# A joint text and image attention block: the text's transposes, text gate and residual moved

## The chip, the core and the metric

The kernel runs on one core of a Trainium2 chip. The core has a matrix engine (TensorE, PE in the profile, with its weight loads as PEld), a vector engine (VectorE, DVE), a scalar engine (ScalarE, ACT), a general engine (GpSimd, POOL) and SyncE (SP), which here only issues DMAs. Sixteen DMA engines move data between device memory and the on-chip memory SBUF; TensorE writes its sums to a second on-chip memory, PSUM. The metric is the time of one execution on the device in microseconds, as the median of several runs.

## The reference

There are 2 batches, each with 256 image tokens and 32 text tokens of width D = 1152. Both streams are normalised and modulated by vectors that come from a condition `c`; they attend to one another jointly; each has an output projection, a gate and a residual. Everything is bf16.

```
mod_i = silu(c) @ wmod_img ; mod_t = silu(c) @ wmod_txt     # shift, scale, gate: the first 3 of 6 blocks of D
hi = layernorm(x_img) * (1 + sci) + shi
ht = layernorm(x_txt) * (1 + sct) + sht
q, k, v = concat(ht @ wqkv_txt, hi @ wqkv_img)              # along the tokens, each of q, k, v
a = softmax(q k^T * D**-0.5) v ;  at, ai = split(a)
out_i = x_img + gai * (ai @ wo_img)
out_t = x_txt + gat * (at @ wo_txt)
```

## The kernel before, in words

D is cut into KT = 9 blocks of 128 rows (index kt or dt). Image tokens form four tiles of 128 (`NIT`), text tokens of both batches together form 64 rows (`NTT`). Fourteen weight blocks of D x D pass through five slots (`w0` to `w4`) in an order written out by hand: `load_w` brings a block in one DMA, `load_rows` in several, cut at rows of 128. All these loads are issued by SyncE, in program order, and each waits until the last reader of its slot is done. `late_loads` issues the last five blocks: image gate, text value, image output (slot 4, rows cut at 3 and 6), text gate, text output (slot 1, cut at row 5).

Most instructions are wrapped in `pin`, which keeps an engine's instructions in program order; those that are not wrapped may be placed by the scheduler.

The order of the work on TensorE is: scale rows and image transposes, image values (`v_open`), shift rows, the image's Q (`qk_img`, block 0) and K (block 1) with hooks at given column blocks j, then the text's Q and K (`qk_txt`), scores, the gate row of the image (`img_gate`), the text's values (`v_txt`), transposes of the softmax, attention (`attn_pair`), and the outputs (`out_img` for four image tiles, `out_txt`).

What the change touches:

- **Text normalisation and transposes.** In the hook at j = 3 of Q, ScalarE takes the text's sums (lines 422 and 423), then `txt_norm` writes the normalised text to `xn_t` in two pieces, 640 and 512 columns, on partitions 0 to 63 and 64 to 127 (line 433). In the hook at j = 1 of K, `txt_transposes` has TensorE transpose five blocks of 128x128 into PSUM (`tr`, line 64), and ScalarE copies them to `xT_t` in two copies (line 441). Between the two hooks VectorE forms the text's shift from 18 long operations on `acc_sh` (lines 451 and 453). `shift_blocks` reduces it, TensorE folds it at j = 7 (`shift_fold`), and `txt_scale` and `txt_shift` make `hT_t`.
- **Gate rows.** `mod_rows` computes a gate's row for both batches in a tiled run: four column groups of 32 stand side by side on TensorE (`tile_position`), so four products run at once. `mod_row_out` has ScalarE copy the row (line 538) and POOL write it to device memory, `gsc` (line 540). POOL then reads it back, spread over the partitions: to `gb` for the image (line 554, `img_gate_spread`), to `gbf` for the text (line 564, in `txt_gate`).
- **Text residual.** `xf` holds the text residual in the layout of the text output; POOL loads it in two DMAs at the end of `img_gate_spread` (line 556).
- **Outputs.** `out_img` computes one image tile in chunks of 384 columns, nine products for each; VectorE multiplies by the gate (line 728) and adds the residual (line 729); a DMA stores the row. It takes a hook, `between`, that is called ahead of its second chunk. `out_txt` computes the text output in two halves of 2 x 288 columns, each with 18 products of 64 columns, two side by side; VectorE multiplies by `gbf` (line 745) and adds `xf` (line 746); two DMAs store it.

The PSUM pool `ps_mm` has six banks, `ps_tr` two. The order of the end is:

```
    C3 = (CH, CH, CH)
    out_img(0, C3)
    out_img(1, C3, between=txt_gate)
    out_img(2, C3)
    out_txt()
    out_img(3, (CH, CH, 224, 160), parts=(2 * CH, D - 160, D))
```

Of the kernel before, what the change touches and what calls it, by code (L numbers as in the profile page):

```python
# [8 lines left out]
ACT = mybir.ActivationFunctionType  # L9
# [5 lines left out]
def kernel(  # L15
# [26 lines left out]
    NTT = B * NT  # L42
    CH = 384
    NCH = D // CH
    VC = 288
# [5 lines left out]
    act = ctx.enter_context(tc.tile_pool(name="act", bufs=1))  # L51
    const = ctx.enter_context(tc.tile_pool(name="const", bufs=1))
    work = ctx.enter_context(tc.tile_pool(name="work", bufs=2))
    small = ctx.enter_context(tc.tile_pool(name="small", bufs=4))
    ps_mm = ctx.enter_context(tc.tile_pool(name="ps_mm", bufs=6, space=PSUM))
    ps_tr = ctx.enter_context(tc.tile_pool(name="ps_tr", bufs=2, space=PSUM))

    pin = tc.keep_in_program_order

    def mm(*a, **k):  # L60
        return pin(nc.tensor.matmul(*a, **k))  # L61

    def tr(*a, **k):
        return pin(nc.tensor.transpose(*a, **k))

    xt_flat = x_txt.rearrange("b n d -> (b n) d")
# [26 lines left out]
    def load_rows(slot, src, c0, cuts=(0, 3, 6)):  # L93
        t = wtile(slot)
        sv = wview(src, c0)
        for r0, r1 in zip(cuts, cuts[1:] + (KT,)):
            nc.sync.dma_start(t[:, r0:r1, :], sv[:, r0:r1, :])  # L97
        return t
# [45 lines left out]
    pb_all = act.tile([P, 2 * B + 1, PBW], bf, name="pb")  # L144
    pb_tiles = [pb_all[:, i, :] for i in range(2 * B)]
    pb_txt = pb_all[:, 2 * B, :]
    KH = (KT + 1) // 2
    xn_t = act.tile([P, KH * P], bf)
    nc.gpsimd.memset(pb_txt, 0.0)
    nc.gpsimd.memset(xn_t[NTT:P, (KT - KH) * P:KH * P], 0.0)  # L150
    nc.gpsimd.memset(pb_all[:, 0:2 * B, NTOK:PBW], 0.0)
    fold = const.tile([P, NGG, LW], bf)
    nc.vector.reduce_max(fold[:, 0, :], ident[:].rearrange("p (g l) -> p l g", g=NGG), axis=AX.X)
# [165 lines left out]
    t3, t0, t6 = [(x_tiles(k0, 1), k0, 1) for k0 in (3, 0, 6)]  # L319
# [39 lines left out]
    for kt in range(KT):  # L359
        for b in range(B):  # L360
            h = hT_i[:, kt, b * NI:(b + 1) * NI]
# [31 lines left out]
    gsc = tc.dram_tile([2, B, D], bf, name="mod_scratch")  # L393
# [20 lines left out]
    xT_t = act.tile([P, KT, NTT], bf)  # L414
# [14 lines left out]
    def txt_norm():  # L429
        rstd = ln_rstd(sm_t[0:NTT, 2:3], NTT, sign=-1.0)  # L430
        pin(nc.scalar.activation(sm_t[0:NTT, 1:2], sm_t[0:NTT, 0:1], ACT.Copy, scale=rstd[0:NTT, :]))
        for h, (c0, c1) in enumerate(((0, KH * P), (KH * P, D))):
            pin(nc.scalar.activation(xn_t[NTT * h:NTT * (h + 1), 0:c1 - c0], x_t[:, c0:c1], ACT.Identity,
                                     bias=sm_t[0:NTT, 1:2], scale=rstd[0:NTT, :]))

    def txt_transposes():
        tpt = ps_tr.tile([P, KH, 2, NTT], bf, tag="tr")
        for k in range(KH):
            tr(tpt[:, k].rearrange("p h t -> p (h t)"), xn_t[:, k * P:(k + 1) * P], ident[:])
        for h, (k0, k1) in enumerate(((0, KH), (KH, KT))):  # L440
            nc.scalar.copy(xT_t[:, k0:k1, :], tpt[:, 0:k1 - k0, h, :])

    acc_sh = act.tile([P, B, D], f32, tag="Bt")

# [91 lines left out]
    def mod_row_out(gps, si):  # L536
        g_sb = work.tile([P, VC], bf, tag="garow")
        pin(nc.scalar.copy(g_sb[:], gps[:]))
        for b in range(B):
            nc.gpsimd.dma_start(gsc[si, b, :].rearrange("(g j) -> g j", g=NGG), g_sb[b:P:32, :])  # L540

    gb = act.tile([P, B, D], bf, tag="Bt")
    gbf = act.tile([P, 2, VC], bf)
# [8 lines left out]
    def img_gate_spread():  # L552
        for b in range(B):
            pin(nc.gpsimd.dma_start(gb[:, b, :], gsc[0, b, :].partition_broadcast(P)))
        for g in range(2):
            pin(nc.gpsimd.dma_start(xf[64 * g:64 * g + NTT, :, :],
                                    xt_flat.rearrange("t (r g j) -> g t r j", r=2, g=2)[g]))

    def txt_gate():
        mod_row_out(mod_rows(w_ga_t), 1)  # L560
        for g in range(2):
            for b in range(B):
                r0 = 64 * g + 32 * b
                nc.gpsimd.dma_start(gbf[r0:r0 + NT, :, :],
                                    gsc[1, b, :].rearrange("(r g j) -> g r j", r=2, g=2)[g].partition_broadcast(NT))

    v_last()
    late = {}

    def late_loads():  # L570
        late["ga_i"] = load_w(0, wmod_img, 2 * D)
        shift_v_spread()
        late["v_t"] = load_w(2, wqkv_txt, 2 * D)
        late["o_i"] = load_rows(4, wo_img, 0)
        late["ga_t"] = load_w(3, wmod_txt, 2 * D)
        late["o_t"] = load_rows(1, wo_txt, 0, (0, 5))

    qk_img(w_q_i, 0, {0: (shift_part(0, 2),), 3: (txt_stats, shift_part(2, 4), txt_var, txt_norm),
                      5: (shift_part(4, 7),), 8: (shift_part(7, KT),)})
# [135 lines left out]
    def out_img(i, chunks, parts=None, between=None):  # L715
        b = i // TPB
        t0 = b * NTOK + qpos[b][i % TPB]
        o = work.tile([P, D], bf, tag="o")
        c0 = s0 = 0
        for n in chunks:  # L720
            if c0 and between:
                between = between()
# [5 lines left out]
            nc.vector.tensor_mul(tmp[:, 0:n], ps[:, 0:n], gb[:, b, c0:c0 + n])  # L728
            nc.vector.tensor_add(o[:, c0:c0 + n], tmp[:, 0:n], x_i[:, i, c0:c0 + n])  # L729
            c0 += n  # L730
            if parts is None and c0 == D or parts and c0 in parts:
                (nc.scalar if parts and c0 == D else nc.sync).dma_start(oi_v[b, i % TPB, :, s0:c0], o[:, s0:c0])
                s0 = c0

    def out_txt():
        of = work.tile([P, 2, VC], bf, tag="of", bufs=1)
        for r in range(2):
            ps = ps_mm.tile([P, VC], f32, tag="mm")
            for dt in range(KT):
                for g in range(2):  # L740
                    c0 = (2 * r + g) * VC
                    mm(ps[64 * g:64 * g + NTT, :], lhsT=aT[:, dt, NI:NI + NTT], rhs=w_o_t[:, dt, c0:c0 + VC],
                       start=(dt == 0), stop=(dt == KT - 1), tile_position=(0, 64 * g))
            tmp = work.tile([P, CH], bf, tag="tmp")
            nc.vector.tensor_mul(tmp[:, 0:VC], ps[:], gbf[:, r, :])
# [12 lines left out]

# [28 lines left out]
```

## Time and profile before

| what | value |
|---|---|
| median of 6 runs | 117.59 us (117.27 to 118.17) |
| the profiled execution: its time | 117.89 us |
| the profiled execution: its span | 115.7 us |
| TensorE busy | 110.4 us, 95% of the span |
| VectorE, ScalarE, POOL busy | 62%, 38%, 10% |
| moved by DMA | 41.02 MB, mean 355 GB/s |
| granted TensorE clock | full, throughout |

The span is the time from the first to the last instruction of the profiled execution; its time on the device has 2.2 us more, which lie around the span. Times in the views are counted from the start of the span. In a timeline a line has start, duration, engine, line of the kernel, operation, tiles as `out<-in`, shape and count; in brackets stands the idle time of the engine ahead of it and what ended it. A `q` behind an engine's name (SPq) marks an instruction of its queue, such as a DMA's issue.

### The profile page before, as it was taken

To read this page: it belongs to the slowest core of one execution; us is meant where nothing else is said; L and a number is where in the kernel's file an instruction comes from. 1 tells how busy PE (TensorE), PEld (TensorE's weight loads), DVE (VectorE), ACT (ScalarE), POOL (GpSimd) and SP (SyncE) were. 2 spreads that over 40 slices of the span, in tenths; PEclk is the share of its full clock that TensorE was granted. 3 is DMA by queue.
4 is the path that set the end of the run, shared out by engine and by line. 5 is a ranking of instruction groups with operands and counts; after the bars stand their busy time and mean duration, and the time that the engine had idled before them with its cause. 6 is when DMAs were issued, how large, how long until landed. Compare 5 with 4: busy or idle time off the path is not lost.

```text
span 115.7 us, 2579 instructions
## 1 busy us (share of the span) xinstructions
PE 110.4 (95%) x1078; PEld 63.8 (55%) x1078; DVE 72.1 (62%) x152; ACT 43.5 (38%) x93; POOL 12.1 (10%) x32
## 2 busy tenths in 40 slices
PE   4999899999999999999999999999999999999990
PEld 2246544445574444444744458887966665557670
DVE  3489492053879997999997040018768409556571
ACT  5799600042653259934323223244656400100000
POOL 7200000000000000000000000003441600407000
PEclk9999999999999999999999999999999999999999
DMA  3999999999999999999999999999999999961223
GB/s 118 355 356 397 401 405 411 411 412 413 410 401 410 305 386 413 408 415 352 412 410 408 411 408 408 335 408 406 415 398 410 407 419 368 410 263 41 112 51 102
DMA packets 18917, 41.02 MB, mean 355 GB/s; under 512 B 1323, under 2 KB 1851, under 8 KB 18907
## 3 DMA queue, kind: packets, MB, share of 16 engines
q1 hardware_dynamic: 18032, 39.85, 90.3%
q0 software_dynamic: 480, 0.89, 2.2%
q10 hardware_dynamic: 395, 0.12, 0.4%
q8 instruction: 8, 0.13, 0.4%
q14 instruction: 2, 0.02, 0.0%
HBM read 39.52 MB, written 1.34 MB: 353 GB/s over the span
## 4 chain that ended last, share of the span: by engine, by line
DMA 52%; SPq 17%; DVE 12%; PE 12%; ACT 2%; issue 2%
DMA t<-in_wmod_img_dram 23%; DMA t<-in_wmod_txt_dram 17%; SPq L97 15%; DMA x_t<-in_x_txt_dram 11%; PE ps L61 11%; DVE acc_sh L453 10%; SPq L108 1%; PE gps L61 1%; ACT junk L422 1%; ACT junk L423 1%; DVE tmp L728 1%; DVE o L729 1%; SPq L104 1%; ACT qkT L379 0%; DVE sm_t L426 0%
## 5 line engine op out<-in xcount | busy, mean ns | idle before, releaser
L61 PE MATMUL ps<-xT_i,t 128*128 128x512 bf16 x162 | 35.7, 379 | 0.0
L61 PEld LDWEIGHTS <-t 128*128 128x128 bf16 x333 | 21.0, 98 | 19.1 <-issue 0.5
L453 DVE SCALAR_TENSOR_TENSOR acc_sh<-t,sTf,acc_sh 128x1152 f32<-128x1152 bf16 x16 | 21.4, 1405 | 0.0
L61 PE MATMUL ps<-t,aT 128*128 128x384 bf16 (+3 forms) x153 | 20.3, 308 | 0.0
L61 PE MATMUL vps<-t,hS_i 128*128 128x512 bf16 (+1 forms) x108 | 17.9, 326 | 0.2 <-DVE hS_i L270 0.2
L61 PEld LDWEIGHTS <-aT 128*128 128x128 bf16 (+1 forms) x153 | 13.0, 101 | 7.1 <-issue 0.8
L61 PEld LDWEIGHTS <-hS_i 128*128 128x128 bf16 x108 | 9.1, 98 | 8.9 <-DVE hS_i L270 0.4
L381 ACT CAST qkT<-ps 128x512 bf16<-128x512 f32 (+2 forms) x11 | 6.1, 551 | 14.9 <-PE ps L61 13.5
L728 DVE TENSOR_TENSOR tmp<-ps,gb 128x384 bf16<-128x384 f32 (+2 forms) x13 | 6.8, 524 | 7.2 <-PE ps L61 7.2
L614 POOL TENSOR_SCALAR pb<-e,rs 128x32 bf16<-128x32 f32 (+1 forms) x5 | 2.3, 456 | 75.8 <-DVE rs L606 75.8
L61 PE MATMUL wps<-warm 128*128 128x512 bf16 x24 | 8.1, 498 | 1.5 <-DVE unit L128 1.5
L379 ACT ACTIVATE qkT<-ps 128x512 bf16<-128x512 f32 (+2 forms) x11 | 6.0, 559 | 7.3 <-PE ps L61 7.2
L178 DVE CAST v_i<-vps 128x512 bf16<-128x512 f32 x5 | 3.5, 691 | 8.0 <-PE vps L61 8.0
L594 DVE TENSOR_REDUCE nmx<-sps 128x1 f32<-128x288 f32 x4 | 1.8, 457 | 9.4 <-PE sps L61 9.4
L180 ACT CAST v_i<-vps 128x512 bf16<-128x512 f32 x4 | 2.3, 580 | 10.2 <-PE vps L61 10.2
L61 PEld LDWEIGHTS <-sT 128*32 128x32 bf16 x180 | 4.6, 96 | 1.9 <-issue 0.7
L61 PEld LDWEIGHTS <-warm 128*128 128x128 bf16 x25 | 2.7, 119 | 5.3 <-issue 2.9
L61 PE MATMUL gps<-t,sT 128*32 128x288 bf16 x144 | 5.2, 287 | 0.2 <-DMA t<-in_wmod_txt_dram 0.2
L61 PE MATMUL sps<-qkT 128*128 128x288 bf16 (+1 forms) x54 | 5.3, 287 | 0.0
L659 DVE TENSOR_SCALAR aT<-aps,svc 128x288 bf16<-128x288 f32 x9 | 4.3, 518 | 1.4 <-PE aps L61 1.4
L61 PE MATMUL aps<-pT,v_i 128*128 128x288 bf16 x36 | 5.1, 287 | 0.0
L729 DVE TENSOR_TENSOR o<-tmp,x_i 128x384 bf16<-128x384 bf16 (+2 forms) x13 | 4.4, 342 | 1.0 <-DMA out_dram<-o 0.6
(112 smaller groups left out, 105.4 us busy)
## 6 DMA issues: line engine op xcount, KB each, us to landing
t<-in_wqkv_txt_dram SPq DMA_DIRECT2D x3, 2592.0 KB, 11.9
t<-in_wmod_img_dram SPq DMA_DIRECT2D x2, 2592.0 KB, 15.4
t<-in_wmod_txt_dram SPq DMA_DIRECT2D x2, 2592.0 KB, 21.3
t<-in_wqkv_img_dram SPq DMA_DIRECT2D x3, 864.0 KB, 14.5
t<-in_wqkv_img_dram SPq DMA_DIRECT2D x1, 2592.0 KB, 16.8
t<-in_wo_img_dram SPq DMA_DIRECT2D x3, 864.0 KB, 12.8
t<-in_wqkv_img_dram SPq DMA_DIRECT2D x3, 576.0 KB, 8.7
t<-in_wmod_txt_dram SPq DMA_DIRECT2D x2, 864.0 KB, 13.4
```

The lines of the kernel that those rows point to most:

```text
L61: return pin(nc.tensor.matmul(*a, **k))
L97: nc.sync.dma_start(t[:, r0:r1, :], sv[:, r0:r1, :])
L178: nc.vector.tensor_copy(out_ap, in_ap)
L180: nc.scalar.copy(out_ap, in_ap)
L379: nc.scalar.mul(out_ap, in_ap, SCALE)
L381: nc.scalar.copy(out_ap, in_ap)
L453: pin(nc.vector.scalar_tensor_tensor(acc, w_sh_t[:, kt, :], col, acc, op0=ALU.mult, op1=ALU.add))
L594: pin(nc.vector.reduce_max(nmx[0:qn, :], sps[0:qn, :], axis=AX.X, negate=True))
L614: pin(nc.gpsimd.tensor_scalar(dst, src, rs[0:qn, :], 0.0, op0=ALU.mult, op1=ALU.add))
L659: nc.vector.tensor_scalar(dst, tiles[(b, dt)][:], bias, None, op0=ALU.add)
L728: nc.vector.tensor_mul(tmp[:, 0:n], ps[:, 0:n], gb[:, b, c0:c0 + n])
L729: nc.vector.tensor_add(o[:, c0:c0 + n], tmp[:, 0:n], x_i[:, i, c0:c0 + n])
```

## The change

It does four things. First, the text is no longer transposed by TensorE: `txt_norm` writes the normalised text in eight pieces of 32 tokens x 288 elements to four groups of 32 partitions, so that one VectorE transpose, which works in blocks of 32x32, gives `xT_t` directly. Second, the text gate is no longer called between chunks of image tile 1: `txt_gate` and `out_txt` now stand together between image tiles 1 and 2, and `out_txt` is cut into products of 32 columns (four side by side, as in the gate row), takes both halves over rows 0 to 4, then 5 and 6, then 7 and 8 of its weights, and accumulates in the two banks of `ps_tr`. The text output's weights are loaded with the same cuts, the image output's with one cut at row 5. Third, the text's gating and store (`out_txt_store`) come after image tile 2; its adds run on POOL. Fourth, POOL loads `xf` behind the write of the text's gate row. The operations concerned are wrapped in `pin`.

```diff
-    KH = (KT + 1) // 2
-    xn_t = act.tile([P, KH * P], bf)
+    xn_t = act.tile([P, KT, B, LW], bf)
     nc.gpsimd.memset(pb_txt, 0.0)
-    nc.gpsimd.memset(xn_t[NTT:P, (KT - KH) * P:KH * P], 0.0)
...
     def txt_norm():
...
-        for h, (c0, c1) in enumerate(((0, KH * P), (KH * P, D))):
-            pin(nc.scalar.activation(xn_t[NTT * h:NTT * (h + 1), 0:c1 - c0], x_t[:, c0:c1], ACT.Identity,
-                                     bias=sm_t[0:NTT, 1:2], scale=rstd[0:NTT, :]))
+        x_g = x_t[:].rearrange("p (k g l) -> p g k l", g=NGG, l=LW)
+        for g in range(NGG):
+            for b in range(B):
+                p0, p1 = NT * b, NT * (b + 1)
+                pin(nc.scalar.activation(xn_t[LW * g:LW * (g + 1), :, b, :], x_g[p0:p1, g], ACT.Identity,
+                                         bias=sm_t[p0:p1, 1:2], scale=rstd[p0:p1, :]))
 
     def txt_transposes():
-        tpt = ps_tr.tile([P, KH, 2, NTT], bf, tag="tr")
-        for k in range(KH):
-            tr(tpt[:, k].rearrange("p h t -> p (h t)"), xn_t[:, k * P:(k + 1) * P], ident[:])
-        for h, (k0, k1) in enumerate(((0, KH), (KH, KT))):
-            nc.scalar.copy(xT_t[:, k0:k1, :], tpt[:, 0:k1 - k0, h, :])
+        pin(nc.vector.transpose(xT_t[:].rearrange("p k t -> p (k t)"), xn_t[:].rearrange("p k b l -> p (k b l)")))
...
     def img_gate_spread():
         for b in range(B):
             pin(nc.gpsimd.dma_start(gb[:, b, :], gsc[0, b, :].partition_broadcast(P)))
+
+    def txt_gate():
+        mod_row_out(mod_rows(w_ga_t), 1)
         for g in range(2):
             pin(nc.gpsimd.dma_start(xf[64 * g:64 * g + NTT, :, :],
                                     xt_flat.rearrange("t (r g j) -> g t r j", r=2, g=2)[g]))
-
-    def txt_gate():
-        mod_row_out(mod_rows(w_ga_t), 1)
         for g in range(2):
             for b in range(B):
                 r0 = 64 * g + 32 * b
-                nc.gpsimd.dma_start(gbf[r0:r0 + NT, :, :],
+                pin(nc.gpsimd.dma_start(gbf[r0:r0 + NT, :, :],
...
-        late["o_i"] = load_rows(4, wo_img, 0)
+        late["o_i"] = load_rows(4, wo_img, 0, (0, 5))
         late["ga_t"] = load_w(3, wmod_txt, 2 * D)
-        late["o_t"] = load_rows(1, wo_txt, 0, (0, 5))
+        late["o_t"] = load_rows(1, wo_txt, 0, (0, 5, 7))
...
     def out_txt():
+        tiles = [ps_tr.tile([P, VC], f32, tag="tr", name="txo") for r in range(2)]
+        for d0, d1 in ((0, 5), (5, 7), (7, KT)):
+            for r, ps in enumerate(tiles):
+                for dt in range(d0, d1):
+                    for g in range(2):
+                        for b in range(B):
+                            c0, r0, t0 = (2 * r + g) * VC, 64 * g + NT * b, NI + NT * b
+                            mm(ps[r0:r0 + NT, :], lhsT=aT[:, dt, t0:t0 + NT], rhs=w_o_t[:, dt, c0:c0 + VC],
+                               start=(dt == 0), stop=(dt == KT - 1), tile_position=(0, r0))
+        return tiles
+
+    def out_txt_store(tiles):
         of = work.tile([P, 2, VC], bf, tag="of", bufs=1)
-        for r in range(2):
-            ps = ps_mm.tile([P, VC], f32, tag="mm")
-            for dt in range(KT):
-                for g in range(2):
-                    c0 = (2 * r + g) * VC
-                    mm(ps[64 * g:64 * g + NTT, :], lhsT=aT[:, dt, NI:NI + NTT], rhs=w_o_t[:, dt, c0:c0 + VC],
-                       start=(dt == 0), stop=(dt == KT - 1), tile_position=(0, 64 * g))
-            tmp = work.tile([P, CH], bf, tag="tmp")
-            nc.vector.tensor_mul(tmp[:, 0:VC], ps[:], gbf[:, r, :])
-            nc.vector.tensor_add(of[:, r, :], tmp[:, 0:VC], xf[:, r, :])
+        for r, ps in enumerate(tiles):
+            tmp = work.tile([P, CH], bf, tag="tmpt")
+            pin(nc.vector.tensor_mul(tmp[:, 0:VC], ps[:], gbf[:, r, :]))
+            pin(nc.gpsimd.tensor_add(of[:, r, :], tmp[:, 0:VC], xf[:, r, :]))
...
     out_img(0, C3)
-    out_img(1, C3, between=txt_gate)
+    out_img(1, C3)
+    txt_gate()
+    txt = out_txt()
     out_img(2, C3)
-    out_txt()
+    out_txt_store(txt)
     out_img(3, (CH, CH, 224, 160), parts=(2 * CH, D - 160, D))
```

More of the change, by code (lines that the diff above doesn't have):

```diff
@@ L539, in mod_row_out @@
         for b in range(B):
-            nc.gpsimd.dma_start(gsc[si, b, :].rearrange("(g j) -> g j", g=NGG), g_sb[b:P:32, :])
+            pin(nc.gpsimd.dma_start(gsc[si, b, :].rearrange("(g j) -> g j", g=NGG), g_sb[b:P:32, :]))
     gb = act.tile([P, B, D], bf, tag="Bt")
@@ L563, in txt_gate @@
                 r0 = 64 * g + 32 * b
-                nc.gpsimd.dma_start(gbf[r0:r0 + NT, :, :],
-                                    gsc[1, b, :].rearrange("(r g j) -> g r j", r=2, g=2)[g].partition_broadcast(NT))
+                pin(nc.gpsimd.dma_start(gbf[r0:r0 + NT, :, :],
+                                        gsc[1, b, :].rearrange("(r g j) -> g r j", r=2, g=2)[g].partition_broadcast(NT)))
     v_last()
@@ L713, with out_img @@
         attn_pair(*[[(b, dt) for dt in dts] for b in range(B)])
-    def out_img(i, chunks, parts=None, between=None):
+    def out_img(i, chunks, parts=None):
         b = i // TPB
@@ L720, in out_img @@
         for n in chunks:
-            if c0 and between:
-                between = between()
             ps = ps_mm.tile([P, CH], f32, tag="mm")
@@ L727, in out_img @@
             tmp = work.tile([P, CH], bf, tag="tmp")
-            nc.vector.tensor_mul(tmp[:, 0:n], ps[:, 0:n], gb[:, b, c0:c0 + n])
-            nc.vector.tensor_add(o[:, c0:c0 + n], tmp[:, 0:n], x_i[:, i, c0:c0 + n])
+            pin(nc.vector.tensor_mul(tmp[:, 0:n], ps[:, 0:n], gb[:, b, c0:c0 + n]))
+            pin(nc.vector.tensor_add(o[:, c0:c0 + n], tmp[:, 0:n], x_i[:, i, c0:c0 + n]))
             c0 += n
```

## The prediction

> **What bounds the kernel now.** I read the page's busy shares and DMA row first, then the timeline of each engine from the text normalisation on, then the DMA issues with their landings. One profiled execution carries the sum: its span is 115.7 us and its time 117.89 us, 0.30 above the median of the six runs (117.59), so I work out a difference in the span and apply it to the median. Half a per cent, 0.59 us, is about what a measurement of this kernel can tell from no change.
>
> ```profile
> PE 110.4 (95%) x1078; PEld 63.8 (55%) x1078; DVE 72.1 (62%) x152; ACT 43.5 (38%) x93; POOL 12.1 (10%) x32
> ...
> DMA  3999999999999999999999999999999999961223
> ```
>
> TensorE is busy for 95% of the span, and so are the DMA engines until the 35th slice, about 101 us. Both are bounds at once: a gain on TensorE counts only as far as the weights arrive earlier too. The text transposes and the tail on TensorE (start, duration), then the weight loads of the tail, and the evictions on ScalarE around the transposes:
>
> ```profile
> 52.58 0.44 PE L64 MATMUL tpt<-ident,xn_t 128*128 128x128 bf16 x5
> ...
> 54.90 1.29 PE L61 MATMUL gps<-t,shT 128*32 128x288 bf16 x36
> 56.01 1.28 PE L61 MATMUL gps<-t,sT 128*32 128x288 bf16 x36
> ...
> 90.80 6.01 PE L61 MATMUL ps<-t,aT 128*128 128x384 bf16 x36
> 97.02 1.29 PE L61 MATMUL gps<-t,sT 128*32 128x288 bf16 x36 [0.21 <-DMA t<-in_wmod_txt_dram]
> ```
>
> ```profile
> 98.24 7.10 PEld L61 LDWEIGHTS <-aT 128*128 128x128 bf16 x45 [0.24 <-issue]
> ...
> 105.66 2.10 PEld L61 LDWEIGHTS <-aT 128*64 128x64 bf16 x36 [0.32 <-issue]
> ...
> 107.98 4.39 PEld L61 LDWEIGHTS <-aT 128*128 128x128 bf16 x36 [0.23 <-issue]
> ```
>
> ```profile
> 50.84 0.60 ACT L379 ACTIVATE qkT<-ps 128x512 bf16<-128x512 f32 x1 [1.35 <-PE ps L61]
> 52.78 0.58 ACT L381 CAST qkT<-ps 128x512 bf16<-128x512 f32 x1 [1.34 <-PE ps L61]
> ...
> 55.00 0.58 ACT L381 CAST qkT<-ps 128x512 bf16<-128x512 f32 x1 [1.03 <-PE ps L61]
> ```
>
> An image product of 384 columns takes (6.01 - 0.33) / 35 = 0.162 us. A tiled run of 36 products of 32 columns, followed by another of its kind, takes 56.01 - 54.90 = 1.11 us. Each change of the tiling leaves a small hole: 45 products (7.30 us) fill the 7.42 us from 98.24 to 105.66, so 0.1 us a change. 36 products from 90.80 end at 96.64, so the text gate, at 97.02, waited some 0.28 us for its weights. ScalarE, waiting for TensorE, gives the pace of the Q and K blocks: 1.94 us from one to the next, 2.22 over the five transposes.
>
> The DMA issues (KB, then us to landing) and the end of VectorE:
>
> ```profile
> 79.17 6.09 SPq L97 DMA_DIRECT2D t<-in_wo_txt_dram  x1
> ...
> t<-in_wo_txt_dram SPq DMA_DIRECT2D x1, 1440.0 KB, 21.2
> t<-in_wo_txt_dram SPq DMA_DIRECT2D x1, 1152.0 KB, 17.9
> xf<-in_x_txt_dram POOLq DMA_DIRECT2D x2, 72.0 KB, 6.9
> gbf<-mod_scratch POOLq DMA_DIRECT2D x4, 36.0 KB, 2.1
> ```
>
> ```profile
> 99.05 1.21 POOL L540 DMA_DIRECT2D mod_scratch<-g_sb  x2 [7.49 <-ACT g_sb L538]
> 104.11 2.16 POOL L564 DMA_DIRECT2D gbf<-mod_scratch  x4 [3.85 <-DMA mod_scratch<-g_sb]
> ```
>
> ```profile
> 107.91 0.46 DVE L745 TENSOR_TENSOR tmp<-ps,gbf 128x288 bf16<-128x288 f32 x1 [1.20 <-DMA gbf<-mod_scratch]
> ...
> 111.12 0.56 DVE L728 TENSOR_TENSOR tmp<-ps,gb 128x384 bf16<-128x384 f32 x1 [0.51 <-PE ps L61]
> 111.71 0.36 DVE L729 TENSOR_TENSOR o<-tmp,x_i 128x384 bf16<-128x384 bf16 x1
> ...
> 112.96 0.24 DVE L729 TENSOR_TENSOR o<-tmp,x_i 128x160 bf16<-128x160 bf16 x1
> ```
>
> The first five row blocks of the text output's weights land at 79.17 + 21.2 = 100.4; the other four are issued behind them, at 79.17 + 6.09, and land 17.9 later at about 103.2, the last weights of the kernel. Today nobody waits for them: the text output starts at 105.66. VectorE ends at 113.20, right behind TensorE; then a store and the closing.
>
> **The change, part by part.**
>
> Transposes. TensorE loses five: 2.22 - 1.94, so 0.28 us goes. VectorE gains one 32x32-block transpose of 128x576 bf16. Not in the trace; the nearest row is the same operation on 128x288 f32, 0.47 us, so between 0.75 (half a fixed cost) and 0.95; I take 0.8. It stands behind the sums of acc_sh, so it delays the blocks' reduction, ready at 61.62 and used by TensorE at 66.94: 5.3 us of cover. Without it the 0.8 would stop TensorE. ScalarE loses two copies (0.71) and normalises in eight pieces of 288 instead of 640 and 512 elements: 0.92 and 0.81 us give 0.85 ns an element and 0.38 fixed, 0.62 a piece, 5.0 instead of 1.75 us. Behind it queue the evictions of the image's Q blocks: the one finished at 45.0 is read at about 51.5 instead of 47.7. There are six banks and a block takes 1.94 us, so its bank is wanted at 54.7; 3 us of cover. The memset on POOL at 2.3 us had no waiter. One limit: the value weights of the text are used at 81.81 and the DMA stream runs without a break, so part of the 0.28 may turn into a wait there; between 0 and 0.28, and the next step makes it indifferent.
>
> Loads. The image output's weights come in two DMAs instead of three, the text output's in three instead of two. Issue time on SP moves, but these DMAs land 13 to 21 us after issue in a backlog; zero. The residual xf (2 x 72 KB) leaves the stream at 90 us: at some 410 GB/s that is 0.36 us, so the last weights come at 102.8 instead of 103.2, the block rows 5 and 6 at 101.4 and rows 0 to 4 at 100.0.
>
> The tiled run. Image output 0 starts at 90.80 - 0.28 = 90.52; now 54 image products (8.76) precede the gate: 99.28, 0.10 for the change of tiling, gate from 99.38 (its weights long landed: the 0.28 of wait goes). Gate 1.11, text from 100.49. Text now has 72 products of 32 columns instead of 36 of 64; at the gate's pace 2.22 us. Both halves over rows 0 to 4 take 1.23 (101.72; landed 100.0), rows 5 and 6 take 0.49 (102.21; landed 101.4), and rows 7 and 8 are reached at 102.21 but land at 102.8. **TensorE waits 0.6 us there**; behind it stands image output 2. Then 0.05 + 0.49 + 0.10: image output 2 from 103.44, plus 27 x 0.162: image output 3 from 107.82 instead of 107.98. So of 0.28 + 0.28 + 0.2 for two changes of tiling, only 0.16 is left; the rest is the stall of the DMA stream, moved from the gate to the last weights.
>
> The gate row's trip. From the gate's last product to landed gbf it takes 9.5 us today (98.3 to 107.8). After: row copied at 101.1, two writes issued at 101.4 and 102.0, then xf's two issues (1.22 us on POOL) until 103.8, then gbf's four (3.7 us from first issue to last landing). The writes' landing decides. Row: 4.6 us under the weights' load; with an empty stream gbf needs 2.1. The Trainium skill, "DMA: Bandwidth & Descriptors", section "Anatomy of one DMA — SWDGE (gpsimd) path", gives about 2.0 us fixed. By the page, landing at 104.1 and gbf at 107.8; by the loaded row, 106.6 and 110.3. The load ends at 102.8, so I take 104.6 and gbf at 108.3. xf's issues lie inside that wait and cost nothing; if the wait were under 1.2 us they would.
>
> VectorE's end. The text multiplies now stand behind image output 2: its last eviction ends at about 108.96, so gbf at 108.3 is in time (today VectorE waited 1.20 for it). Two multiplies 0.96: 109.92; chunk 0 of image 3 (0.93) 110.85; chunk 1 is ready at 110.96; from there as today, 0.16 earlier: end at 113.04. (Image 2's row buffer waits for image 0's store, landed by 104.0 today; its first add now comes at 105.7, so nothing.) The text's two adds (0.62) leave VectorE for POOL: this pays for the later place. VectorE is full here, 4.03 us of work in 4.08.
>
> POOL's adds: 128x288 with two inputs, not in the trace. Its one-input rows are 0.47 us for 128x32 and 0.52 for 64x96, some 0.8 ns an element: at least 0.67. By two inputs at the page's pace (below) about 0.8 to 1.05. The text store waits for them (about 111.2), lands some 2.4 later at 113.6, before the last image store (114.8): zero by itself. But here a rule speaks against the change. Row first: VectorE's adds of 0.36 us at 104.9 and 106.4 kept that length while POOL issued DMAs. The Trainium skill, "SBUF — State Buffer", section "Who interferes with whom", says that a VectorE instruction with two SBUF inputs contends with a GpSimd instruction that reads SBUF, the first holding the shared ports to its end; "GPSIMD Engine Reference", section 3, has about 2.6 cycles an element for a two-input operation, 0.63 us on 288. The two adds would hold the port from 109.5 to E, and chunk 0's add (due 110.5) would wait until then; the end is E + 2.5. By the row: no cost, 113.04. By the rule with 0.8 us each, E = 111.1: 113.6. I take the row for the forecast, and keep 0 to +1.1.
>
> Sum: 0.16 earlier on TensorE and at the end: 115.7 - 0.15, so **117.59 - 0.15 = 117.44 us**.
>
> **The rivals.**
>
> 1. The forecast (36%): about 117.4, own range 117.0 to 117.9: the last weights are the bound before and after.
>
> 2. The last rows land early (24%): if they come by 102.2, TensorE gains the whole 0.28 + 0.28 + 0.2 = 0.8: image 3 from 107.2, VectorE's end at 112.4: 116.8; by half, 117.1. For it: the landing is that of the slowest engine, and gb's and xf's traffic at 93 to 97 us may have cost more than its bytes. Against: the DMA row has no idle slice to take up.
>
> 3. The port lock (26%), which ends slower: price E + 2.5 - 113.04. It decides from adds of 0.55 us each on: 0.7 each gives +0.4 against the forecast, 0.8 gives +0.6, 1.05 gives +1.1; so 117.8 to 118.5, at 118.0 for the middle. For it: the rule, and VectorE without slack. Against: no row shows it.
>
> 4. The gate row is late (14%): if the writes take their loaded 4.6 us, gbf lands at 110.3, and 0.96 + 0.93 + 0.92 + 0.66 + 0.56 behind it end at 114.3: 118.7. It decides from a landing of gbf at 109.0 on. Against: the load ends under way.
>
> **How the numbers follow.** The likeliest is 117.4. Faster by over 0.59 (under 117.0): three quarters of case 2 and a sixth of case 1, 0.24. Slower by over 0.59 (over 118.18): case 4, half of case 3 and a tenth of case 1, 0.31. Between: 0.45. The range takes case 2's full gain and most of case 3: 116.8 to 118.4; what is left out is mainly case 4.
>
> **What would show it.** Right: no product tpt; a wait of TensorE for in_wo_txt_dram inside the text output at about 102 us, 0.3 to 0.9 long; no wait of the gate for in_wmod_txt_dram; image 3 from about 107.8; VectorE's text multiplies straight behind image 2; a POOL add of 0.7 to 1.0 us. Case 2: no such wait. Case 3: an L729-like add of 128x384 well over 0.36 us beside POOL's. Case 4: the text multiply waits for gbf past 109. Wrong altogether: a wait of TensorE near 55 or 67 us (the normalisation or the transpose on the path), or text products slower than 0.03 us each.

## The result, and the profile after

The changed kernel takes 117.0 us (median of 34 runs, 116.21 to 118.19); the kernel before, on the same chips, 117.38 us (71 runs, 116.83 to 118.46). The ratio is 0.9962, with a 95% interval of 0.9948 to 0.9976: 0.44 us less (0.28 to 0.61). Measured once more, the same kernel gave 0.9943 (0.9911 to 0.9975, e11 below). Both intervals exclude 1, so there is a gain, and it is small: about the half per cent that the forecast took as what a measurement can tell.

The profiled execution of the new kernel has a span of 115.2 us and a time of 117.31. Its busy shares and the DMA row:

```profile
PE 109.5 (95%) x1109; PEld 63.1 (55%) x1109; DVE 72.2 (63%) x151; ACT 45.9 (40%) x97; POOL 13.2 (11%) x33
...
DMA  3999999999999999998999999999999999963043
```

TensorE lost 0.9 us of busy time and is still at 95%; the DMA engines are still full to the 35th slice. The text's normalisation and transpose on ScalarE and VectorE, then TensorE over the same time (timelines; start, duration):

```profile
46.10 5.09 ACT L434 ACTIVATE xn_t<-x_t,sm_t,rstd 32x288 bf16<-32x288 bf16 x8
51.22 2.06 ACT L377 ACTIVATE qkT<-ps 128x512 bf16<-128x512 f32 x4
...
58.30 0.76 DVE L438 STREAM_TRANSPOSE xT_t<-xn_t 128x576 bf16<-128x576 bf16 x1
```

```profile
43.82 11.17 PE L61 MATMUL ps<-xT_i,t 128*128 128x512 bf16 x51
```

Eight pieces took 5.09 us, the evictions behind them (`qkT<-ps`, which empty TensorE's sums out of PSUM) resumed at 51.22 and made up four in a row; TensorE has no wait there. The tail on TensorE:

```profile
90.82 8.94 PE L61 MATMUL ps<-t,aT 128*128 128x384 bf16 x54
99.69 1.29 PE L61 MATMUL gps<-t,sT 128*32 128x288 bf16 x36
100.80 2.38 PE L61 MATMUL txo<-t,aT 128*32 128x288 bf16 x72
103.11 8.97 PE L61 MATMUL ps<-t,aT 128*128 128x384 bf16 x63
```

No line carries a bracket, so no wait for weights is named at the gate or in the text output. From the text's first product to image tile 2 it is 2.31 us, 72 products at the gate's pace (2.22) and a change of tiling (0.1), so there is no hidden wait either. The stall that the forecast placed here did not come. The last weights of the kernel (KB, us from issue to landing; issued at 88.72) and POOL's queue:

```profile
t<-in_wo_txt_dram SPq DMA_DIRECT2D x1, 576.0 KB, 13.6
```

```profile
101.72 1.15 POOL L537 DMA_DIRECT2D mod_scratch<-g_sb  x2 [11.13 <-ACT g_sb L535]
102.86 1.23 POOL L556 DMA_DIRECT2D xf<-in_x_txt_dram  x2
104.29 2.12 POOL L561 DMA_DIRECT2D gbf<-mod_scratch  x4 [0.20 <-issue]
109.11 1.42 POOL L747 TENSOR_TENSOR of<-tmp,xf 128x288 bf16<-128x288 bf16 x2 [2.71 <-DVE tmp L746]
```

The last weights landed at 88.72 + 13.6 = 102.3. TensorE reached their rows after 56 of the 72 text products, at 100.80 + 56 x 0.031 = 102.5: 0.2 us of room. VectorE's end:

```profile
108.31 0.36 DVE L724 TENSOR_TENSOR o<-tmp,x_i 128x384 bf16<-128x384 bf16 x1
108.58 0.81 DVE L746 TENSOR_TENSOR tmp<-txo,gbf 128x288 bf16<-128x288 f32 x2
109.31 0.55 DVE L723 TENSOR_TENSOR tmp<-ps,gb 128x384 bf16<-128x384 f32 x1
109.89 0.85 DVE L724 TENSOR_TENSOR o<-tmp,x_i 128x384 bf16<-128x384 bf16 x1
110.67 0.54 DVE L723 TENSOR_TENSOR tmp<-ps,gb 128x384 bf16<-128x384 f32 x1
...
112.48 0.24 DVE L724 TENSOR_TENSOR o<-tmp,x_i 128x160 bf16<-128x160 bf16 x1
```

The multiplies follow image tile 2 without a wait for `gbf`. One add, at 109.89, took 0.85 us instead of 0.36: it runs beside POOL's two adds (109.11 to 110.53).

**A ruler for the experiments.** The start of the first Q product varies from 32.6 to 33.7 us over the profiles, whatever the kernel, and moves all that follows on TensorE. So I measure from it (the line `ps<-xT_i,t`; 33.16 before, 33.46 after) to the end of VectorE's last add, and split that at the start of image tile 2: *front* is TensorE and its waits, *back* is image tiles 2 and 3 with VectorE's end. Front and back are differences of starts and ends in timelines like those above. One thing the ruler does not take out: the weights do not move with Q one for one. In e8 Q starts 0.79 us earlier than in after (32.67), but the last weights land only 0.5 earlier (101.8), so TensorE meets the end of the stream sooner in a profile with an early Q.

| kernel | front | back | sum | ratio to before (95%) |
|---|---|---|---|---|
| before | | | 80.04 | 1 |
| after | 69.65 | 9.61 | 79.26 | 0.9962 (0.9948 to 0.9976) |
| after, again (e11) | 69.66 | 9.61 | 79.27 | 0.9943 (0.9911 to 0.9975) |
| e1: transposes alone | | | 79.99 | 0.9992 (0.9973 to 1.0011) |
| e9: e1, `gbf` early | | | 80.00 | 0.9994 (0.9968 to 1.0021) |
| e2: tail alone | 70.07 | 9.61 | 79.68 | 0.9990 (0.9972 to 1.0008) |
| e5: `xf` early | 70.37 | 9.61 | 79.98 | 1.0009 (0.9987 to 1.0031) |
| e6: cut at 5 only | 70.00 | 9.62 | 79.62 | 0.9996 (0.9972 to 1.0021) |
| e7: 576 KB more | 71.65 | 9.61 | 81.26 | 1.0134 (1.0103 to 1.0166) |
| e3: adds on VectorE | 69.81 | 9.81 | 79.62 | 0.9991 (0.9969 to 1.0013) |
| e8: four more POOL adds | 69.75 | 9.89 | 79.64 | 0.9983 (0.9965 to 1.0000) |
| e10: five POOL memsets | 70.78 | 9.61 | 80.39 | 0.9971 (0.9952 to 0.9989) |
| e4: 64 columns | 69.78 | 9.61 | 79.39 | 0.9969 (0.9949 to 0.9988) |
| e12: value weights earlier | 69.66 | 9.62 | 79.28 | 0.9984 (0.9963 to 1.0005) |

In before and e1 and e9 the text comes behind image tile 2, so they are not split. The sum is one execution; the ratio is many, each taken beside its own runs of before. e11 and e12, with after's front and back to 0.01 us, have ratios of 0.9943 and 0.9984: ratios from different comparisons that lie 0.002 to 0.003 apart do not tell two kernels apart. By the ruler the change is worth 0.78 us, which is the whole 0.28 (transposes) + 0.28 (the gate's wait) + 0.2 (two changes of tiling). By the clock it is 0.44. The two profiled spans differ by 0.48 (115.68 and 115.20), since Q started 0.30 later in after's. The profiled executions were 0.5 (before) and 0.3 us (after) above their medians; how often the gate of before waits as long as in that profile was not measured.

### The profile page after: what moved, and what is told of

Read it like the earlier page. It is cut to its first block, busy times and chain, and to the rows that moved or that the text cites. A ratio compares the mean times of both kernels' runs of the same rounds, so it can differ in the third digit from the quotient of the medians.

```text
span 115.2 us, 2644 instructions
## 1 busy us (share of the span) xinstructions
PE 109.5 (95%) x1109; PEld 63.1 (55%) x1109; DVE 72.2 (63%) x151; ACT 45.9 (40%) x97; POOL 13.2 (11%) x33
## 4 chain that ended last, share of the span: by engine, by line
PE 77%; DMA 11%; SPq 4%; DVE 4%; issue 1%; DVEq 0%
PE ps L61 48%; PE vps L61 12%; DMA t<-in_wqkv_img_dram 11%; PE gps L61 5%; PE aps L61 5%; PE sps L61 4%; PE txo L61 2%; DVE tmp L723 2%; SPq L110 2%; SPq L108 2%; DVE o L724 2%; PE pT_ps L64 1%; SPq L104 1%; DVE tmp L746 1%; PE shps L61 0%
## 5 line engine op out<-in xcount | busy, mean ns | idle before, releaser
L61 PE MATMUL ps<-t,aT 128*128 128x384 bf16 (+2 forms) x117 | 17.9, 314 | 0.0
L61 PE MATMUL wps<-warm 128*128 128x512 bf16 x24 | 7.6, 471 | 1.5 <-DVE unit L128 1.5
L724 DVE TENSOR_TENSOR o<-tmp,x_i 128x384 bf16<-128x384 bf16 (+2 forms) x13 | 4.9, 380 | 0.4
```

The costliest lines, as they stand in the source:

```text
L724: pin(nc.vector.tensor_add(o[:, c0:c0 + n], tmp[:, 0:n], x_i[:, i, c0:c0 + n]))
```

## The experiments

### Which part brings the gain: e1, e2, e9

e1 is the kernel before with the new normalisation and transpose alone (the cut shows the transpose; `txt_norm` and `xn_t` are changed as in the whole diff):

```diff
...
-        for k in range(KH):
-            tr(tpt[:, k].rearrange("p h t -> p (h t)"), xn_t[:, k * P:(k + 1) * P], ident[:])
-        for h, (k0, k1) in enumerate(((0, KH), (KH, KT))):
-            nc.scalar.copy(xT_t[:, k0:k1, :], tpt[:, 0:k1 - k0, h, :])
+        pin(nc.vector.transpose(xT_t[:].rearrange("p k t -> p (k t)"), xn_t[:].rearrange("p k b l -> p (k b l)")))
```

> The kernel before with one part of the change alone: VectorE transposes the text, TensorE's five transposes are gone. Theory 1 (two bounds): TensorE arrives 0.28 us earlier at the text gate, but its weights land at 97.0 as before, so the wait there grows from 0.28 to about 0.56 us and the time stays, 0 to -0.1 us. Theory 2 (TensorE alone is the bound, the wait in the one profile before was an accident of that execution): the full -0.28 us. Theory 3 (eight small ScalarE pieces or VectorE's 0.76 us transpose cost something): slower, with a wait of TensorE near 55 or 67 us.

e2 is the complement: the new kernel with the five TensorE transposes and two copies put back (the diff above, reversed).

> The change without the transposes: TensorE transposes the text as before, the rest is the changed kernel. Theory 1 (two bounds): the gate no longer waits for its weights (up to 0.28 us) and two changes of tiling fall away (0.2 us), so -0.3 to -0.45 us, nearly the whole of the change. Theory 2 (TensorE alone): only the 0.2 us of tiling changes, so -0.15 to -0.2 us, and the rest of the change's -0.44 is the transposes'.

Neither alone is resolved from before: 0.9992 and 0.9990, while both together give 0.9962 (and 0.9969 in e4 below, measured beside the same runs of before as e1 and e2). e2's 0.1 us is less than either theory said. But the clock does not settle it: the transposes' 0.28 us would be a ratio of 0.9976, which lies inside e1's interval. What follows is read from one profile of each. By the ruler the tail alone brings 0.36 us and the transposes alone 0.05. Yet in e1 TensorE did gain: its gate began 63.33 us from the first Q product (96.09 - 32.76) instead of 63.86 (97.02 - 33.16), the transposes' 0.28 and a wait for weights that this profile does not have (the first theory had it grow to 0.56). But VectorE gave it back (e1, timelines of TensorE, POOL and VectorE):

```profile
96.09 1.29 PE L61 MATMUL gps<-t,sT 128*32 128x288 bf16 x36
...
98.12 1.21 POOL L537 DMA_DIRECT2D mod_scratch<-g_sb  x2 [6.96 <-ACT g_sb L535]
104.00 2.16 POOL L561 DMA_DIRECT2D gbf<-mod_scratch  x4 [4.67 <-DMA mod_scratch<-g_sb]
...
108.40 0.46 DVE L742 TENSOR_TENSOR tmp<-ps,gbf 128x288 bf16<-128x288 f32 x1 [2.62 <-DMA gbf<-mod_scratch]
```

The write of the gate's row, issued at 98.7, landed only at 103.9. Before, it was issued at 99.7 and landed at 104.1; after, issued at 102.3, it landed at 104.2. So the landing hardly depends on the issue; it comes 1 to 2 us after the last weights (102.7, 103.15 and 102.3). After's alone would not show this, since it lands 1.9 us behind its issue; e7 below moves the end of the stream and not the issue. VectorE waited 2.62 us instead of 1.20, in front of image tile 3's evictions. To see whether that wait is the whole answer, e9 is e1 with it removed: it reads the gate of the image, written earlier, in place of that of the text, and so leaves out the right text output:

```diff
-                                    gsc[1, b, :].rearrange("(r g j) -> g r j", r=2, g=2)[g].partition_broadcast(NT))
+                                    gsc[0, b, :].rearrange("(r g j) -> g r j", r=2, g=2)[g].partition_broadcast(NT))
```

> The kernel of the transposes alone, with gbf read from the image's gate row, which lies in device memory long before, so its four loads do not wait for the text row's write (the text output is gated by the wrong row; all else is computed). In the transposes alone TensorE ended 0.53 us earlier than before, counted from the start of Q, but VectorE waited 2.62 us for gbf and its end came only 0.05 us earlier. Theory 1 (the gate row's trip, whose write lands only behind the weight stream, eats the transposes' gain): gbf lands by about 104, VectorE does not wait, and the time falls by 0.3 to 0.5 us against the transposes alone. Theory 2 (the gain is lost at the weight stream's end itself, or there is none): the same time as the transposes alone.

The ratio is 0.9994: still nothing. The wait for `gbf` is gone, and another stands in the profile (e9, timelines of TensorE and VectorE):

```profile
96.46 1.29 PE L61 MATMUL gps<-t,sT 128*32 128x288 bf16 x36 [0.35 <-DMA t<-in_wmod_txt_dram]
...
106.43 0.46 DVE L742 TENSOR_TENSOR tmp<-ps,gbf 128x288 bf16<-128x288 f32 x1 [0.26 <-PE ps L61]
```

TensorE waits for the gate's weights, and its gate begins 63.82 us from the first Q product (96.46 - 32.64), as late as before's 63.86. So in these profiles of the old order a faster TensorE meets the weight stream at the gate, or `gbf` at VectorE, and each alone is enough to take the gain. In the new order neither meeting occurs, and after's gate begins 0.29 us earlier from Q than e2's (66.23 and 66.52): there the transposes count on TensorE. That they count for nothing in the time of the old order is not shown: e9's interval, too, holds 0.9976.

### The stream of weights: e5, e6, e7

e5 moves the loads of `xf` back to where they were, ahead of the weights' end:

```diff
     def img_gate_spread():
         for b in range(B):
             pin(nc.gpsimd.dma_start(gb[:, b, :], gsc[0, b, :].partition_broadcast(P)))
-
-    def txt_gate():
-        mod_row_out(mod_rows(w_ga_t), 1)
         for g in range(2):
             pin(nc.gpsimd.dma_start(xf[64 * g:64 * g + NTT, :, :],
                                     xt_flat.rearrange("t (r g j) -> g t r j", r=2, g=2)[g]))
+
+    def txt_gate():
+        mod_row_out(mod_rows(w_ga_t), 1)
```

> The changed kernel with one thing undone: the residual xf (2 x 72 KB) is loaded behind the image gate's spread again, inside the weight stream. In the changed kernel TensorE reaches the last weight rows at 102.5 and they land at 102.3, and in five profiles so far they land at 102.0 to 102.3 with xf late and at 102.7 to 103.2 with it early. Theory 1 (xf's traffic held the weights up): they land 0.4 to 0.9 us later, TensorE waits 0.2 to 0.6 us for them inside the text output, and the time is 0.2 to 0.5 us longer. Theory 2 (by bytes alone): 0.36 us later, a wait of about 0.1 us, hardly to be measured. Theory 3 (the landing has other causes): no wait, no difference.

The gain is gone: the interval of 1.0009 is apart from both of the new kernel's. Here is the stall that was forecast (e5, timeline of TensorE):

```profile
100.03 1.89 PE L61 MATMUL txo<-t,aT 128*32 128x288 bf16 x56
102.44 0.67 PE L61 MATMUL txo<-t,aT 128*32 128x288 bf16 x16 [0.52 <-DMA t<-in_wo_txt_dram]
103.05 3.26 PE L61 MATMUL ps<-t,aT 128*128 128x384 bf16 x19
```

The front is 0.72 longer than after's, the back is equal. Over the profiles, the last weights landed at 102.4 to 103.2 with `xf` early (before, e1, e5, e9), and at 102.0 to 102.3 with it late (after, e2, e3, e4, e11, e12), with 101.8 in e8, 102.6 in e6 and 103.2 in e10. The means are some 0.65 apart, where the bytes had given 0.36. Three of the four early ones are of the old order, so the cleanest pair is e5 and e8, which differ ahead of the text's store in the place of `xf` alone, start Q at the same time (32.68 and 32.67) and were measured beside the same runs of before: 102.4 against 101.8.

Why 0.6 and not 0.36? The profile shows it from 95 to 98 us, when `xf` lands if it is early (e5, then after; the last two figures are the busy share of the DMA engines and GB/s):

```profile
95.00:98.00 3.00, 3.00 (x20) 1.78 (x19) 2.86 (x8) 0.00 (x0) 0.00 (x0) 1.00 1.05 359
```

```profile
95.00:98.00 3.00, 3.00 (x21) 1.79 (x19) 2.19 (x5) 0.00 (x0) 0.00 (x0) 1.00 1.03 406
```

The engines are as busy and move less. With `xf` early it is 370, 350, 359 and 316 GB/s (before, e1, e5, and e9, whose `gbf` falls there too), with it late 404 to 414 in all ten others. Against 410, e5 loses 51 GB/s x 3 us = 153 KB, or 0.37 us, on top of the 0.36 for `xf`'s own bytes: by this estimate 0.7. Why the engines are slower beside `xf` stays open.

Late `xf` does not keep TensorE wholly clear of the stream. The text output took 2.31 us in after, e11 and e12, but 2.40 to 2.46 in e2, e3, e8 and e10, where rows 7 and 8 began 0.04 us behind the last landing: a wait of about 0.1 us that no bracket names.

e6 takes away the cut at row 7, so that rows 5 to 8 come in one DMA:

```diff
-        late["o_t"] = load_rows(1, wo_txt, 0, (0, 5, 7))
+        late["o_t"] = load_rows(1, wo_txt, 0, (0, 5))
```

> The changed kernel with the text output's weights in two DMAs (rows 0 to 4, 5 to 8) as before, so rows 5 and 6 are known to be there only when 7 and 8 are. TensorE needs row 5 at 102.0 and it now lands with the last at 102.3: a wait of about 0.25 us in the middle of the text output, and 0 to +0.25 us on the time. If the stream's end has room (theory of no bound by DMA), no wait.

It gave 0.9996. TensorE stops at row 5, and the front is 0.35 longer, of which the profile names 0.16 as idle (e6, timeline):

```profile
101.04 1.40 PE L61 MATMUL txo<-t,aT 128*32 128x288 bf16 x40
102.61 1.16 PE L61 MATMUL txo<-t,aT 128*32 128x288 bf16 x32 [0.16 <-DMA t<-in_wo_txt_dram]
```

From start to start it comes out: 40 products at 0.031 would have brought row 5 to 102.27, and it began at 102.61, 0.34 later.

e7 puts an unused load of 576 KB ahead of the text output's weights:

```diff
+        more = act.tile([P, 2, D], bf, name="more")
+        nc.sync.dma_start(more[:], wview(wo_txt, 0)[:, 0:2, :])
         late["o_t"] = load_rows(1, wo_txt, 0, (0, 5, 7))
```

> The changed kernel with one extra load of 576 KB ahead of the text output's weights on SyncE's queue, which nobody reads. At about 410 GB/s it takes 1.4 us of the stream. Theory 1 (the weight stream's end is a second bound, with about 0.25 us of room): the last rows land at about 103.7, TensorE waits about 1.1 to 1.2 us for them, and the time grows by about 1.1 us. Theory 2 (TensorE alone bounds): the same time, or less than 0.3 us more.

The time rose to 118.87, 1.66 us above before's 117.21 beside it. The front is 2.0 us longer than after's, where about 1.1 was expected: 1.55 of it lie at the text output, for some 1.4 us of stream (576 KB at 410 GB/s), and 0.45 ahead of it, with a wait of 0.26 for the text's value weights, which stand ahead of the extra load in the queue. At the text output (e7, timelines of TensorE and POOL):

```profile
101.06 2.16 PE L61 MATMUL txo<-t,aT 128*32 128x288 bf16 x56 [0.17 <-DMA t<-in_wo_txt_dram]
103.96 0.67 PE L61 MATMUL txo<-t,aT 128*32 128x288 bf16 x16 [0.74 <-DMA t<-in_wo_txt_dram]
```

```profile
101.63 1.15 POOL L537 DMA_DIRECT2D mod_scratch<-g_sb  x2 [11.43 <-ACT g_sb L535]
...
105.85 2.12 POOL L561 DMA_DIRECT2D gbf<-mod_scratch  x4 [1.85 <-DMA mod_scratch<-g_sb]
```

The gate row's writes were issued as in after (101.63 and 101.72), and POOL could read the row back only at 105.85, not at 104.29. So it is the end of the stream that decides when they land.

The end of the stream is thus a second bound, a few tenths of a microsecond behind TensorE. With e5 it is shown from both sides: more bytes ahead of the last weights cost their time or more, and the place of 144 KB decides whether the change gains. Not undone alone were the gate's place between the image tiles, the `pin`s and the cut of the image output's weights.

### POOL's adds and the shared port: e3, e8, e10

e3 gives the text's adds back to VectorE:

```diff
-            pin(nc.gpsimd.tensor_add(of[:, r, :], tmp[:, 0:VC], xf[:, r, :]))
+            pin(nc.vector.tensor_add(of[:, r, :], tmp[:, 0:VC], xf[:, r, :]))
```

> The changed kernel with the text's two residual adds on VectorE instead of POOL. In the changed kernel's profile VectorE's add of image 3's first chunk took 0.85 instead of 0.36 us beside POOL's adds. If the two engines share a port, this add is 0.36 again. VectorE gets 0.62 us of adds and loses 0.49 us of blocking: its end moves by about +0.1 us, so no difference in time (0 to +0.2 us). If POOL's help is worth its whole 0.62 us, +0.5 us.

In e3 image tile 3's first add is back at 0.36 us (timeline of VectorE):

```profile
109.55 0.55 DVE L723 TENSOR_TENSOR tmp<-ps,gb 128x384 bf16<-128x384 f32 x1
110.14 0.36 DVE L724 TENSOR_TENSOR o<-tmp,x_i 128x384 bf16<-128x384 bf16 x1
```

So the 0.49 us more is the price of POOL's adds beside it. Still e3's back is 0.20 longer: two adds on VectorE (0.62 for the pair) cost more than the collision. Its ratio is 0.9991, worse in the middle than after's, with intervals that just overlap. (0.16 of the sum's 0.36 lies in the front, at the edge of the stream, and is not the adds'.)

e8 asks what further collisions would cost: four unused adds on POOL behind the two.

```diff
             pin(nc.gpsimd.tensor_add(of[:, r, :], tmp[:, 0:VC], xf[:, r, :]))
+        junk = work.tile([P, 2, VC], bf, tag="junk2", bufs=1)
+        for n in range(4):
+            pin(nc.gpsimd.tensor_add(junk[:, n % 2, :], of[:, n % 2, :], xf[:, n % 2, :]))
```

> The changed kernel with four more adds on POOL behind the two of the text output, of the same size, from SBUF to SBUF, into a buffer that nobody reads. If POOL's reads and the second SBUF input of a VectorE add share a port, the adds of image 3's chunks 1 to 3 are drawn out beside them as chunk 0's was (0.85 instead of 0.36 us), by up to 0.7 us each, and the end of VectorE moves out by 1 to 2 us. If the 0.85 us had another cause (the DMA issue, the pinned order), they stay at 0.36, 0.27 and 0.24 us and the time stays.

The timelines of POOL and VectorE in e8 show:

```profile
109.81 3.10 POOL L750 TENSOR_TENSOR junk<-of,xf 128x288 bf16<-128x288 bf16 x4
...
110.56 0.36 DVE L724 TENSOR_TENSOR o<-tmp,x_i 128x384 bf16<-128x384 bf16 x1
...
111.25 0.38 DVE L724 TENSOR_TENSOR o<-tmp,x_i 128x224 bf16<-128x224 bf16 x1
...
111.90 0.41 DVE L724 TENSOR_TENSOR o<-tmp,x_i 128x160 bf16<-128x160 bf16 x1
```

The last two adds took 0.38 and 0.41 instead of 0.27 and 0.24, and the back is 0.28 longer. I had expected 1 to 2 us. The add of 128x384 at 110.56 kept its 0.36 although POOL was at work; POOL's own adds, 0.73 alone, stretched to 0.84 and 0.90. So it is not always VectorE that waits. By the starts, the one that came later paid: POOL's add at 109.81 (0.84) began inside VectorE's of 109.20, and the one at 110.61 (0.90) 0.05 us behind VectorE's of 110.56, while VectorE's adds at 109.20, 111.25 and 111.90 began inside a POOL add. e10 writes on POOL without reading:

```diff
             pin(nc.gpsimd.tensor_add(of[:, r, :], tmp[:, 0:VC], xf[:, r, :]))
+        junk = work.tile([P, 2 * VC], bf, tag="junk2", bufs=1)
+        for n in range(5):
+            pin(nc.gpsimd.memset(junk[:], 0.0))
```

> The changed kernel with five memsets of 128x576 on POOL behind the text's two adds, which write into a buffer that nobody reads and read nothing. With four more adds at this place VectorE's last two adds took 0.38 and 0.41 instead of 0.27 and 0.24 us. If it is the reading that collides with the second SBUF input of VectorE's adds, they are 0.27 and 0.24 here; if any access of POOL does, they are drawn out here too.

The same two timelines in e10:

```profile
111.18 3.11 POOL L750 MEMSET junk<- 128x576 bf16 x5
...
111.95 0.36 DVE L724 TENSOR_TENSOR o<-tmp,x_i 128x384 bf16<-128x384 bf16 x1
...
112.65 0.28 DVE L724 TENSOR_TENSOR o<-tmp,x_i 128x224 bf16<-128x224 bf16 x1
...
113.19 0.24 DVE L724 TENSOR_TENSOR o<-tmp,x_i 128x160 bf16<-128x160 bf16 x1
```

Beside the memsets VectorE's adds keep their length to 0.01 us, and the back is 9.61 as without them. (e10's long front is another matter: in that profile the text's values waited 0.80 us for their weights.)

### Small terms: e4 and e12

e4 keeps the new order but makes the text's products 64 columns wide, as before, so that the tiling changes between gate and text:

```diff
-                        for b in range(B):
-                            c0, r0, t0 = (2 * r + g) * VC, 64 * g + NT * b, NI + NT * b
-                            mm(ps[r0:r0 + NT, :], lhsT=aT[:, dt, t0:t0 + NT], rhs=w_o_t[:, dt, c0:c0 + VC],
-                               start=(dt == 0), stop=(dt == KT - 1), tile_position=(0, r0))
+                        c0 = (2 * r + g) * VC
+                        mm(ps[64 * g:64 * g + NTT, :], lhsT=aT[:, dt, NI:NI + NTT], rhs=w_o_t[:, dt, c0:c0 + VC],
+                           start=(dt == 0), stop=(dt == KT - 1), tile_position=(0, 64 * g))
```

> The changed kernel with the text output in products of 64 columns as before, at its new place behind the gate. If what counts is that no change of tiling lies between gate and text, there is a hole of 0.1 to 0.2 us in TensorE's timeline between them, and the time is 0.1 to 0.2 us longer. If the width does not matter (the text run itself takes 2.2 us either way), no difference.

The step from gate to text is 100.64 - 99.42 = 1.22 us instead of 1.11, the 0.1 of a change of tiling, and the front is 0.13 longer. The times do not resolve it (0.9969 beside 0.9962).

e12 takes up the wait for the text's value weights that the profiles of e7 and e10 show: it issues those weights ahead of the load of the value shift.

```diff
-        shift_v_spread()
         late["v_t"] = load_w(2, wqkv_txt, 2 * D)
+        shift_v_spread()
```

> The changed kernel with one more swap in the late loads: the text's value weights are issued ahead of the four spreads of the value shift (4 x 36 KB), not behind them. In the profiles so far the text's value products start 1.10 us behind the image gate row's start when their weights are there, and up to 2.18 us behind it when not (0.80 us of wait for in_wqkv_txt in the worst). The spreads are 0.36 us of the stream at 410 GB/s and are read only at 83.5. If this landing is now the tightest point of the weight stream, the waits of up to 0.36 us there go, and the time falls by 0 to 0.2 us against the changed kernel; by nothing in executions that did not wait. If the spreads then come too late for VectorE's first use, slower.

It gave 0.9984, not better than the new kernel, with the same front. e11 is the new kernel unchanged, once more, on the chip of e9 and e10:

> The changed kernel once more, unchanged, on the same chip as the two others: 0.3 to 0.5 us less than before. It is there so that the experiments that differ by 0.3 us are not read against one measurement alone.

It repeated the gain (0.9943) and the ruler's figures to 0.01 us. None of the variants is shown to be faster than the changed kernel.

## Why the prediction was right in its number and wrong in its stall

**The number.** 117.4 was said, 117.0 was measured, within the range. The change was forecast at 0.15 us and measured at 0.44 (0.28 to 0.61), three times as much, on a base (the median of six runs, 117.59) that came out 0.21 lower over 71. The mechanism that came is that of rival 2, the last rows landing early, which was given 24%; so the nearness of 117.4 is partly luck: the changes in play are small beside the whole.

**The transposes (held).** 0.28 us on TensorE; the VectorE transpose took 0.76 (0.8 said) and ended at 59.06, with `ub` ready at 62.4 before TensorE needed it near 67; the eight pieces took 5.09 (5.0 said), the evictions resumed at 51.22 (51.5 said). What the profiles of e1 and e9 add is that in the old order another wait can take these 0.28 back.

**The tiled run (held, but for its stall).** Gate to text 1.11, as said; two holes of tiling and the gate's wait gone. The forecast's stall of 0.6 us at rows 7 and 8 is the step that failed: TensorE reached them at 102.5, not 102.2, and they had landed at 102.3, not 102.8.

**The residual's bytes (mis-sized; this is the cause).** 144 KB by 410 GB/s gave 0.36 us and a landing at 102.8. Late `xf` was worth about 0.6 in the landings, and 0.5 in the time, give or take 0.3: 0.9962 against e5's 1.0009. Rival 2 had named the reason, that `xf`'s traffic may have cost more than its bytes; the rate of 359 instead of 406 GB/s bears it out. Also the sum took one execution's landing, 103.2, as fixed, whereas it varied from 102.4 to 103.2 among kernels with `xf` early, and TensorE's own start came 0.3 later in the profile of after. On a margin of a few tenths that decides between a stall and none.

**The gate row's trip (held).** The writes landed at 104.2 (104.6 said, between estimates of 104.1 and 106.6) and `gbf` at 107.9, in time; `xf`'s two issues on POOL fitted inside the wait. Rival 4 did not come, for the reason given against it: the landing follows the end of the stream, as e7 shows.

**The port (the rule held, its price was absorbed).** The row chosen for the forecast, adds unharmed beside DMA issues, was the wrong one to go by, as rival 3 had it: an add beside POOL's adds took 0.85. The Trainium skill, "SBUF — State Buffer", section "Who interferes with whom", was right that a two-input VectorE instruction contends with a GpSimd one that reads SBUF and not with one that only writes (e10). That the first holds the ports to its end, as the prediction has it, is more than the traces show: VectorE's add, 0.36 alone, ended 0.21 behind POOL's last (110.74 and 110.53), so it was not held up to that end (as far as POOL's ends, rough in a profile, tell). POOL's adds took 0.73 each, on which the rival put about 0.4 us. They cost the forecast's end nothing, since they ended at 110.53, not 111.1: the multiplies began right at image tile 2's end and took 0.81, not 0.96. And chunk 1's multiply started at 110.67, about when TensorE had it ready: the multiply of image tile 2's third chunk, 27 products in, started at 107.71, and 18 products of 0.162 later it is 110.63. The forecast's distance from image tile 2 to VectorE's end, 113.04 - 103.44 = 9.60, is the 9.61 of the table.

## What to carry to other kernels

Where two bounds lie within a few tenths of a microsecond of each other, price an edit in pairs: remove the wait at one place, and look at which transfer the engine then meets. A load that nobody needs before the end belongs behind the last load on which the bound engine waits, even if it is only 144 KB. Here a small write into a full DMA stream landed only after the stream's end, so work that hangs on such a write is best placed after that; issuing it earlier gained little.

## What the runs showed of the hardware

- Under the weights' stream, a gate row's write of some 2 KB landed at 103.9, 104.1 and 104.2 us when issued at 98.7, 99.7 and 102.3 (e1, before, after), and with the stream's end moved out (e7) POOL read it back 1.56 us later than in after.
- While 144 KB issued by POOL landed among the weights, the DMA engines moved 316 to 370 GB/s (95 to 98 us; before, e1, e5, e9) at the same busy share, and 404 to 414 in the ten runs without it.
- A VectorE add of 128x384 with both inputs in SBUF took 0.85 instead of 0.36 us beside POOL adds that read SBUF, and kept 0.36 beside POOL memsets (e10). In e8 one add of 128x384 kept 0.36 while POOL's stretched from 0.73 to 0.84 and 0.90: the one that began later was slowed.
- A TensorE wait is longer than its named idle time: in e6 0.16 us is named and the rows begin 0.34 late; in e5 it is 0.52 and 0.68 (100.03 + 56 x 0.031 = 101.76, begun at 102.44).
